# Where the weight conversions of an FNet and hard-swish kernel stand at its start: moving them behind the input's fold and beside the first steps

## The chip, the cores and the metric

One core of a Trainium2 chip. The metric is the device time of one execution in microseconds (us). Executions of one kernel here mostly agree within 0.4%; "fast" means that no execution was disturbed by a lower clock. Ratios are, throughout, the mean time of one kernel's fast runs over the mean of the kernel before's fast runs of the same rounds on the same chip, so they are not quite the ratio of the medians that stand beside them. Times within an execution ("at 100.2 us") are counted from the start of the profiled span.

## The reference

```python
X = np.fft.fft(np.fft.fft(x, axis=1), axis=2).real          # x: (8, 3008, 256) float32
h = X.reshape(24064, 256) @ w_in                            # w_in: (256, 2048) float64
g = h * np.clip(h + 3.0, 0.0, 6.0) / 6.0
out = g @ w_out                                             # w_out: (2048, 256) float64
```

The weights arrive as float64. The kernel reads them as pairs of 32-bit words and makes float32 of them itself.

## The kernel before

The batch is worked in four pairs of sequences. For the first pair this happens in order: the **fold** (eight chunks; GpSimd adds each row to its mirror row, VectorE completes the sums, TensorE applies the first transform, ScalarE copies it to `z`, which goes to DRAM); the load of `g` from there and the **second transform**; then the **steps**, each made of a first product with `w_in`, the activation on VectorE and ScalarE, a combination on GpSimd and a second product with seven matrices `G` made of `w_out`. There are eight steps to a chunk of columns and 384 in all.

The weights come in sixteen pieces, converted two at a time. Eight **conversion pairs** are numbered 0 to 7 in order of use. Pairs 0, 1, 3 and 4 belong to `w_in` and end in a product on TensorE; pairs 2, 5, 6 and 7 belong to `w_out` and end in four operations of GpSimd that fill `G`. One conversion pair goes through every engine:

```python
def narrow_a(j):
    ...
    ts(ex[:], hi, 20, 0x7FF, op0=AL.logical_shift_right, op1=AL.bitwise_and)          # VectorE
    nc.scalar.activation(exf, ex[:], AF.Relu, bias=bias[:, 0:1], scale=1.0)           # ScalarE, three times
    nc.scalar.activation(exf, exf, AF.Relu, bias=bias[:, 1:2], scale=-1.0)
    nc.scalar.activation(ex[:], exf, AF.Identity, bias=bias[:, 2:3], scale=-2.0 ** 23)
    ts(top[:], hi, 0xFFFFF, 0x100000, op0=AL.bitwise_and, op1=AL.bitwise_or)          # VectorE again
    ...
def narrow_b(j):
    st, hi, ex, frac = raw.pop(j)
    nc.vector.scalar_tensor_tensor(ex[:], hi, -2 ** 31, ex[:], op0=AL.bitwise_and, op1=AL.bitwise_or)
    o = st[:].bitcast(F32)[:, 0:WB]
    eng = nc.vector if j < 6 else nc.gpsimd
    eng.tensor_tensor(o, frac, ex[:].bitcast(F32), op=AL.mult)
    w[PIECES[j]] = o
def mix_w_out(j):                                   # a pair of w_out
    ...
    tt(g[3], b11, b12, op=AL.subtract)              # GpSimd, four times
    tt(g[5], b22, g[3], op=AL.add)
    ...
    nc.scalar.mul(g[5], g[5], -1.0)
def fold_w_in(n):                                   # a pair of w_in
    ...
    for blk in range(2):
        ps = bank([P, WB], "wps")
        for i in range(2):
            nc.tensor.matmul(ps[:], C[:, i, blk * P:(blk + 1) * P], ws[i], start=(i == 0), stop=(i == 1))
        nc.scalar.copy(W1[:, blk, cs], ps[:])
    ...                                             # and WN, from sixteen narrow matmuls
```

The main order of the start, before (cut):

```python
narrow_pair(0); use_pair(0)
for c in range(NXC):                                # the fold
    fold(first, c, 0, nc.gpsimd)
    fold(first, c, 1, nc.vector)
    if c + 3 < NXC:
        load_x(first, c + 3)                        # a direct load, then a gather of mirror rows, both on GpSimd
    if c in (2, 5):
        narrow_pair((c + 1) // 3)                   # pairs 1 and 2
    for i in range(XC // 2):
        stage1(first, c, i)
    ...                                             # loads of later pieces and of T
    if c in (2, 5):
        use_pair((c + 1) // 3)
load_g(first, 0); load_g(first, 1); load_t(1)
narrow_pair(3)
...                                                 # second transform
use_pair(3)
...                                                 # pairs 4 to 7 beside steps 0, 1, 3, 5
```

So the seven pairs after pair 0 stand in three places: **two in the fold, one in the gap** between the last `z` and the first step, **four beside the steps**. I write this as 2/1/4.

## Time and profile before

| kernel before | |
|---|---|
| time, median of 3 (range) | 2081.8 us (2078.97 to 2082.96) |
| profiled span, mean clock | 2078.6 us, 0.975 |
| fold of chunk 0 / 3 / 6 / 7 starts on GpSimd | 18.3 / 39.8 / 70.8 / 73.1 us |
| last `z` issued | 85.0 us |
| first VectorE operation of the first step ("first s") | 106.89 us |
| last GpSimd operation into `G` ("last G") | 179.11 us |
| first s to last G | 72.2 us |

The prediction shows the lines that carry this. A line of a timeline reads: start, length, engine, line of the kernel, operation, output<-input, shape, how many were merged, and in brackets the idle time of the engine before it and what ended that. Two more views matter later. The first is VectorE's timeline at the end of one chunk's fold, in the kernel before:

```profile
49.18 0.68 DVE L158 TENSOR_TENSOR y<-xt 94x508 f32<-94x508 f32 x1
49.78 2.27 DVE L159 TENSOR_TENSOR y<-xt 94x8 f32<-94x8 f32 x1
51.98 1.57 DVE L157 TENSOR_TENSOR y<-xt 94x508 f32<-94x508 f32 x1
```

An operation on 8 elements a partition took 2.27 us. The median of its eight executions on VectorE is 0.165 us. The second is the table of busy time by stretch, whose columns are stretch, length, then busy us (and instructions) of TensorE, its weight loads, VectorE, ScalarE, GpSimd, then the granted clock, the DMA share and GB/s:

```profile
100.00:130.00 30.00, 18.37 (x71) 10.65 (x70) 12.16 (x22) 10.13 (x17) 10.03 (x10) 0.82 0.22 64
130.00:165.00 35.00, 25.35 (x102) 21.19 (x101) 25.50 (x47) 17.02 (x29) 20.80 (x23) 0.86 0.25 73
```

While pairs 4 to 7 stand beside the steps, no engine is full and the clock is below 1.

A matmul is called **cold** here and in the prediction where the trace has it at about twice the time that it takes at full clock. The first half of the product at 119.88 us, after a wait of 8.62 us, took 3.97 us at a clock of 0.50; the second half, after a wait of 0.68 us, took 1.98 us at 1.00. **Full clock** is a granted clock of 1.00, as from 208 to 260 us: there four matmuls of 128x256 took 1.03 us, and two of 94x512 were 0.86 us ahead of the next operation, 0.43 each.

### The profile page before, as it was taken

The numbers are of one execution on the slowest core, as the hardware profiler recorded it, in microseconds if no ns is written. First come the engines' busy times: TensorE is split into PE (matmuls) and PEld (weight loads), VectorE is DVE, ScalarE is ACT, GpSimd is POOL, SyncE is SP. The second block draws the span as 40 slices with busy tenths as digits, with TensorE's granted clock in tenths as the row PEclk, the third lists the DMA queues.
The fourth block names the chain that finished last, engine by engine and source line by source line (L and its number), as shares of the span: only waits on it lengthen the run. The fifth ranks groups of instructions, "written<-read, shape, count | busy, mean of one in ns | idle before, by whom it ended". The sixth has DMA issues, their size and how long they took to land.

```text
span 2078.6 us, 28133 instructions
## 1 busy us (share of the span) xinstructions
PE 1974.6 (95%) x9136; PEld 1692.0 (81%) x9136; DVE 1456.9 (70%) x2714; ACT 706.1 (34%) x1205; POOL 1496.1 (72%) x1662
## 2 busy tenths in 40 slices
PE   4468999999999999999999999999999999999997
PEld 1246888888888888888888888888888888888886
DVE  5366676776777677677677677677777777777775
ACT  2344333333333333333333333333333323333332
POOL 6248777877667887788667778778766766766765
PEclk7688999999999999999999999999999999999999
DMA  6420211221110122212111112211110011011000
GB/s 188 142 86 15 57 49 34 50 47 33 29 31 23 44 51 51 51 33 54 29 21 34 43 34 48 51 43 47 31 36 11 17 23 21 18 24 21 16 16 18
DMA packets 158161, 86.81 MB, mean 42 GB/s; under 512 B 132512, under 2 KB 145056, under 8 KB 158016
## 3 DMA queue, kind: packets, MB, share of 16 engines
q1 hardware_dynamic: 129856, 60.28, 12.7%
q0 software_dynamic: 28160, 24.73, 4.5%
q8 instruction: 74, 1.21, 0.3%
q14 instruction: 71, 0.58, 0.1%
HBM read 47.65 MB, written 37.22 MB: 41 GB/s over the span
## 4 chain that ended last, share of the span: by engine, by line
PE 91%; DVE 4%; DMA 2%; ACT 1%; issue 1%; POOL 1%; SPq 0%; DVEq 0%; POOLq 0%; ACTq 0%
PE acc L320 53%; PE v L266 16%; PE u L266 15%; PE ps L193 2%; PE ps L221 2%; PE wps L446 1%; PE ps L237 1%; DVE a L298 1%; DMA st<-in_moe_w_in_dram 1%; ACT t L295 1%; DVE u L279 0%; DVE ex L406 0%; DVE s L271 0%; PE wns L451 0%; DMA g<-zd 0%
## 5 line engine op out<-in xcount | busy, mean ns | idle before, releaser
L310 POOL TENSOR_TENSOR c<-a 128x512 f32<-128x512 f32 (+1 forms) x384 | 479.2, 1248 | 406.7 <-DVE a L298 258.7
L320 PE MATMUL acc<-c,G 128*128 128x256 f32 (+1 forms) x3072 | 714.1, 375 | 0.0
L320 PEld LDWEIGHTS acc<-c,G 128*128 128x128 f32 x3072 | 579.3, 191 | 73.8 <-POOL c L310 0.2
L295 ACT ACTIVATE t<-u,half 128x512 f32<-128x512 f32 (+2 forms) x416 | 272.3, 655 | 1074.8 <-DVE u L279 1063.2
L271 DVE SCALAR_TENSOR_TENSOR s<-qn,WN,u 128x256 f32<-128x256 f32 x768 | 334.4, 477 | 392.2 <-PE u L266 391.9
L320 PE MATMUL acc<-a,G 128*128 128x256 f32 (+1 forms) x2304 | 553.6, 377 | 0.0
L320 PEld LDWEIGHTS acc<-a,G 128*128 128x128 f32 x2304 | 436.8, 191 | 57.3
L266 PE MATMUL v<-q,W 128*128 128x256 f32 x1536 | 398.8, 382 | 17.9 <-DVE a L298 17.9
L266 PE MATMUL u<-q,W 128*128 128x256 f32 x1536 | 394.5, 379 | 0.0
L266 PEld LDWEIGHTS v<-q,W 128*128 128x128 f32 x1536 | 291.3, 191 | 64.3 <-issue 21.9
L266 PEld LDWEIGHTS u<-q,W 128*128 128x128 f32 x1536 | 287.4, 190 | 65.3 <-issue 20.9
L298 DVE SCALAR_TENSOR_TENSOR a<-t,u 128x512 f32<-128x512 f32 (+2 forms) x416 | 265.9, 646 | 105.3 <-ACT t L295 101.0
L310 POOL TENSOR_TENSOR c<-a,c 128x256 f32<-128x256 f32 (+1 forms) x384 | 275.0, 716 | 30.1
L310 POOL TENSOR_TENSOR c<-c,a 128x256 f32<-128x256 f32 (+1 forms) x384 | 275.0, 716 | 30.1
L279 DVE TENSOR_TENSOR u<-s,v 128x512 f32<-128x512 f32 (+1 forms) x384 | 263.0, 685 | 42.6 <-PE v L266 2.5
L295 ACT ACTIVATE t<-v,half 128x512 f32<-128x512 f32 (+1 forms) x384 | 257.0, 669 | 5.3 <-DVE v L285 4.4
L285 DVE TENSOR_TENSOR v<-v,s 128x512 f32<-128x512 f32 (+1 forms) x384 | 257.7, 671 | 1.1
L298 DVE SCALAR_TENSOR_TENSOR a<-t,v 128x512 f32<-128x512 f32 (+1 forms) x416 | 255.1, 619 | 0.1
L310 POOL TENSOR_TENSOR r<-w,e 128x256 f32<-128x256 f32 (+1 forms) x96 | 92.3, 982 | 3.8
L193 PE MATMUL ps<-y,F 94*96 94x512 f32 x120 | 67.0, 656 | 26.2 <-DVE y L159 20.1
L326 ACT ACTIVATE e<-acc 128x512 f32<-128x512 f32 (+1 forms) x192 | 87.0, 543 | 2.9 <-PE acc L320 2.8
L346 DVE STREAM_TRANSPOSE o<-r 128x256 f32<-128x256 f32 (+1 forms) x192 | 72.4, 415 | 6.5 <-POOL r L310 6.4
(70 smaller groups left out, 826.7 us busy)
## 6 DMA issues: line engine op xcount, KB each, us to landing
out_dram<-o SPq DMA_DIRECT2D x736, 32.0 KB, 1.6
zd<-z SPq DMA_DIRECT2D x32, 384.0 KB, 3.0
g<-zd SPq DMA_DIRECT2D x48, 256.0 KB, 4.2
xt<-in_x_dram POOLq DMA_DIRECT2D x28, 376.0 KB, 3.9
st<-in_moe_w_in_dram SPq DMA_DIRECT2D x8, 512.0 KB, 4.4
st<-in_moe_w_out_dram SPq DMA_DIRECT2D x8, 512.0 KB, 5.7
T<-in_c_stage_dram SPq DMA_DIRECT2D x12, 128.0 KB, 7.2
xt<-in_x_dram POOLq DMA_DIRECT2D x4, 282.0 KB, 3.4
```

The source lines that it names most:

```text
L193: nc.tensor.matmul(ps[0:PZ], F[0:PR, 0:PZ], y[:, 2 * i:2 * i + 2, :], start=True, stop=True)
L221: nc.tensor.matmul(ps[:, blk, 2 * u:2 * u + 2], g[:, kk, blk * P:(blk + 1) * P], T[:, :, gr, blk, kk], start=True, stop=True)
L266: nc.tensor.matmul(ps[:, i], W1[:, blk, f * P:(f + 1) * P], q[:, blk, of:of + KC], start=True, stop=True)
L271: nc.vector.scalar_tensor_tensor(s[:, i].rearrange("p k n -> p (k n)"), qn[:, of * N2:(of + KC) * N2], WN[:, f:f + 1], u[:, i].rearrange(" ...
L279: nc.vector.tensor_tensor(u[:, :, 0:ns], s[:, :, 0:ns], v[:, :, 0:ns], op=AL.add)
L285: nc.vector.tensor_tensor(v[:, :, 0:nm], v[:, :, 0:nm], s[:, :, 0:nm], op=AL.subtract)
L295: nc.scalar.activation(t, h, AF.Relu, bias=half[:], scale=scale)
L298: nc.vector.scalar_tensor_tensor(dst, t, 1.0, h, op0=AL.min, op1=AL.mult)
L310: nc.gpsimd.tensor_tensor(out, in0, in1, op=AL.add)
L320: nc.tensor.matmul(ch.acc[i // 2][:, i % 2, 0:ch.n], G[:, i, fc, :], mv, start=(fc == 0 and i % 2 == 0), stop=(fc == NF - 1), skip_group_c ...
L326: nc.scalar.mul(ch.e[:, k:i + 1, 0:ch.n], ch.acc[i // 2][:, 0:i + 1 - k, 0:ch.n], 1.0 / WS)
L346: nc.vector.transpose(o[:, 0:n // DH, h], ch.r[:, m, h, 0:n].rearrange("p (j i) -> p j i", i=DH))
```

## The change

The intent: let the fold run at the speed of its loads alone. No conversion stands in it any more, only three of the weight pieces after the first pair are loaded beside it, and the direct load of `x` leaves GpSimd for SyncE, in 96 rows instead of 94. Pairs 1 and 2 move into the gap, and pair 3 moves past the first step, behind each step's own work: 0/2/5. The multiplications of pieces 2 to 5 go from VectorE to GpSimd. A changed sign of the sixth product saves ScalarE's multiplication by -1.

```diff
-PROD = ("P1", "P2", "-P4", "P5", "P7", "P6", "P3")
+PROD = ("P1", "P2", "-P4", "P5", "P7", "-P6", "P3")
@@ load_forward, the direct half of load_x
+        nr, eng = (PR + 2, nc.sync) if pr.p == 0 else (PR, nc.gpsimd)
+        rows = x_pn[pr.p * PR:pr.p * PR + nr]
@@ finish
-        add(wn[:, 0], e[:, 0], e[:, 5])
+        nc.gpsimd.tensor_tensor(wn[:, 0], e[:, 0], e[:, 5], op=AL.subtract)
@@ narrow_b
-        eng = nc.vector if j < 6 else nc.gpsimd
+        eng = nc.vector if j < 2 else nc.gpsimd
@@ mix_w_out
-        nc.scalar.mul(g[5], g[5], -1.0)
@@ the start
     for c in range(NXC):
         fold(first, c, 0, nc.gpsimd)
+        if c + 3 < NXC:
+            load_partners(first, c + 3)
         fold(first, c, 1, nc.vector)
-        if c + 3 < NXC:
-            load_x(first, c + 3)
-        if c in (2, 5):
-            narrow_pair((c + 1) // 3)
         for i in range(XC // 2):
             stage1(first, c, i)
-        for j in {0: (2, 3), 2: (4,), 3: (5,), 5: (6,), 6: (7,), 7: (8, 9)}.get(c, ()):
-            load_w(j)
+        if c + 3 < NXC:
+            load_forward(first, c + 3)
         if c == 4:
             load_t(0)
-        if c in (2, 5):
-            use_pair((c + 1) // 3)
+            load_w(2)
+        if c == 5:
+            load_w(3)
+            load_w(4)
+    narrow_pair(1)
+    use_pair(1)
     ... load_w(5), load_w(6); load_g(first, 0), load_g(first, 1), load_t(1) ...
-    narrow_pair(3)
+    narrow_pair(2)
+    use_pair(2)
     ... second transform ...
-    use_pair(3)
@@ beside the steps
-            for i, t in enumerate((0, 1, 3, 5)):
-                ... load_w, load_t, narrow_pair(4 + i), use_pair(4 + i) ahead of step t's work
+            for i, t in enumerate((0, 1, 1, 3, 4)):
+                after.setdefault(t, []).extend([(narrow_pair, (3 + i,)), (use_pair, (3 + i,))])
+                ... load_w; all of it behind step t's work
```

More of the change, by code (lines that the diff above doesn't have):

```diff
@@ L116, in __init__ @@
             self.p = p
-            self.x, self.y, self.z = {}, {}, {}
+            self.x, self.xr, self.y, self.z = {}, {}, {}, {}
             self.zd = None
@@ L125, in x_tile, with load_forward, load_partners @@
             pool, tag = ((apool, "a"), (cpool, "c"), (spool, "t"))[(i >= 8) + (i >= 11)]
-        return pool.tile([PR, XC, D], F32, tag=tag, name="xt")
+        return pool.tile([PR + 2, XC, D], F32, tag=tag, name="xt")
     def load_x(pr, c):
-        xt, xr = x_tile(pr, 2 * c), x_tile(pr, 2 * c + 1)
-        rows = x_pn[pr.p * PR:(pr.p + 1) * PR]
+        load_forward(pr, c)
+        load_partners(pr, c)
+    def load_forward(pr, c):
+        xt = x_tile(pr, 2 * c)
+        nr, eng = (PR + 2, nc.sync) if pr.p == 0 else (PR, nc.gpsimd)
+        rows = x_pn[pr.p * PR:pr.p * PR + nr]
         n = XC if c < NXC - 1 else XC - 1
-        nc.gpsimd.dma_start(out=xt[:, 0:n, :], in_=rows[:, c * XC + 1:c * XC + 1 + n, :])
+        eng.dma_start(out=xt[0:nr, 0:n, :], in_=rows[:, c * XC + 1:c * XC + 1 + n, :])
         if n < XC:
-            nc.gpsimd.dma_start(out=xt[:, n:XC, :], in_=rows[:, 0:1, :])
+            eng.dma_start(out=xt[0:nr, n:XC, :], in_=rows[:, 0:1, :])
+        pr.x[c] = xt
+    def load_partners(pr, c):
+        xr = x_tile(pr, 2 * c + 1)
+        pr.xr[c] = xr
         i = pr.p * NXC + c
         nc.gpsimd.indirect_dma_start(
-            out=xr[:].rearrange("p n d -> p (n d)"), out_offset=None, in_=x_r,
+            out=xr[0:PR].rearrange("p n d -> p (n d)"), out_offset=None, in_=x_r,
             in_offset=bass.IndirectOffsetOnAxis(ap=IX[:, i:i + 1], axis=0),
         )
-        pr.x[c] = xt, xr
     def fold(pr, c, part, eng):
-        xt, xr = pr.x[c]
+        xt, xr = pr.x[c][0:PR], pr.xr[c][0:PR]
         n = XC if c < NXC - 1 else XC - 1
@@ L165, in fold @@
             eng.tensor_copy(y[:, n, 0:P + 1:P], xt[:, n, 0:P + 1:P])
-        del pr.x[c]
+        del pr.x[c], pr.xr[c]
     starting = [True]
@@ L476 @@
         fold(first, c, 0, nc.gpsimd)
+        if c + 3 < NXC:
+            load_partners(first, c + 3)
         fold(first, c, 1, nc.vector)
-        if c + 3 < NXC:
-            load_x(first, c + 3)
-        if c in (2, 5):
-            narrow_pair((c + 1) // 3)
         for i in range(XC // 2):
             stage1(first, c, i)
-        for j in {0: (2, 3), 2: (4,), 3: (5,), 5: (6,), 6: (7,), 7: (8, 9)}.get(c, ()):
-            load_w(j)
+        if c + 3 < NXC:
+            load_forward(first, c + 3)
         if c == 4:
             load_t(0)
-        if c in (2, 5):
-            use_pair((c + 1) // 3)
+            load_w(2)
[4 more added lines that the diff above has]
+    use_pair(1)
+    for j in (5, 6):
+        load_w(j)
     load_g(first, 0)
@@ L492 @@
     load_t(1)
-    narrow_pair(3)
+    narrow_pair(2)
+    use_pair(2)
+    for j in (7, 8):
+        load_w(j)
     for i in range(2):
@@ L503 @@
     NST = 2 * NF
+    after = {}
     def beside(p):
@@ L512, in beside @@
         if p == 0:
-            for i, t in enumerate((0, 1, 3, 5)):
-                for j in (10, 11, 12, 13, 14, 15)[2 * i:2 * i + 2]:
-                    put(t, load_w, j)
-                if i + 2 < NG:
-                    put(t, load_t, i + 2)
-                put(t, narrow_pair, 4 + i)
-                put(t, use_pair, 4 + i)
+            for i, t in enumerate((0, 1, 1, 3, 4)):
+                after.setdefault(t, []).extend([(narrow_pair, (3 + i,)), (use_pair, (3 + i,))])
+                for j in range(9 + 2 * i, min(11 + 2 * i, 16)):
+                    after[t].append((load_w, (j,)))
+            for gr in range(2, NG):
+                after.setdefault(gr - 1, []).append((load_t, (gr,)))
             put(NF - 1, close_w)
@@ L573 @@
         mlp2(*chunk(s))
+        for f, a in after.get(s, ()):
+            f(*a)
         if fc == NF - 1:
```

## The prediction

> **What bounds the kernel now.** I read first the busy slices of the page (the span in 40 slices of 52 us; PE is TensorE, POOL is GpSimd, PEclk the clock granted to TensorE).
>
> ```profile
> PE   4468999999999999999999999999999999999997
> POOL 6248777877667887788667778778766766766765
> PEclk7688999999999999999999999999999999999999
> ```
>
> From the fifth slice to the last TensorE is full at full clock. The change touches nothing there, so it can only gain or lose in the first four slices. Next, the table of busy time by stretch: in 0 to 208 us TensorE is busy 124.6 us (21.7 + 25.0 + 34.5 + 43.4) at clocks of 0.74, 0.63, 0.84 and 0.87. In full-clock work there is less: by 187 us four folds of w_in (8 x 0.43 + 1.7 = 5.1 us each), 32 matmuls of the first transform (0.43 each, 13.8), the second transform (3.5), nine first halves of a step (1.73) and seven second halves (3.02): 20.5 + 13.8 + 3.5 + 15.6 + 21.1 = 74.5 us. So 187 - 74.5 = 112 us is the most a perfect start could give back. A gain over 2% needs 41.6 us of it.
>
> Where it goes is in the timeline of GpSimd, line by line (start, length, instruction, idle before and its releaser; L151 is the first instruction of a chunk's fold):
>
> ```profile
> 18.27 1.26 POOL L151 TENSOR_TENSOR xt<-xt 94x508 f32<-94x508 f32 x1 [8.06 <-DMA xt<-in_x_dram,IX]
> 39.78 1.50 POOL L151 TENSOR_TENSOR xt<-xt 94x508 f32<-94x508 f32 x1 [6.43 <-DMA xt<-in_x_dram,IX]
> 66.86 1.11 POOL L433 TENSOR_TENSOR G<-st 128x256 f32<-128x256 f32 x1 [13.85 <-DVE st L409]
> 70.83 1.25 POOL L151 TENSOR_TENSOR xt<-xt 94x508 f32<-94x508 f32 x1
> ```
>
> Chunks 0 and 3 wait for the gather of their partner rows. Chunk 6 waits in GpSimd's order behind a converted weight piece, which came late. Then TensorE's timeline around the step machinery:
>
> ```profile
> 95.44 3.75 PE L221 MATMUL ps<-T,g 128*128 128x128 f32 x16 [11.36 <-DMA g<-zd]
> 105.66 1.11 PE L266 MATMUL u<-q,W 128*128 128x256 f32 x4
> 119.88 3.97 PE L446 MATMUL wps<-st,C 128*128 128x512 f32 x4 [8.62 <-POOL st L409]
> 145.47 2.05 PE L266 MATMUL v<-q,W 128*128 128x256 f32 x4 [5.88 <-DVE a L298]
> 162.87 2.05 PE L266 MATMUL v<-q,W 128*128 128x256 f32 x4 [3.77 <-DVE a L298]
> 180.32 2.05 PE L266 MATMUL v<-q,W 128*128 128x256 f32 x4 [4.88 <-DVE a L298]
> ```
>
> The first step starts at 105.7, and each of the four pairs of weight pieces converted beside steps 0 to 5 costs TensorE a hole. The last is over at 182.2; from there it never waits. The time of the kernel is therefore the moment at which this start is over.
>
> One line of ScalarE shows what the changed sign is for: it multiplies G by -1 after GpSimd's third addition, and the step's relu stands behind it.
>
> ```profile
> 143.62 0.42 ACT L437 ACTIVATE G<-G 128x256 f32<-128x256 f32 x1 [1.57 <-POOL G L435]
> 143.94 0.67 ACT L295 ACTIVATE t<-u,half 128x512 f32<-128x512 f32 x1
> ```
>
> [...] in the undisturbed stretch from 200 to 600 us the direct 94-row load lands in a median 3.9 us, the gather of as many bytes in 11.7. So 96 rows on SyncE are harmless, and the gather stays slow. [...] four matmuls took 2.05 us after a hole against 1.03 otherwise. [...] the second L406 of a pair took 1.23 us against 0.68 while GpSimd multiplied.
>
> **The change part by part.**
>
> *Fold.* Removed ahead of the folds: weight pieces 2 and 3 (1 MB at 25 us) and the conversion of two pairs. The forward load leaves GpSimd: its issue cost 0.57 + 0.3 a chunk, so the cadence falls from 5.04 to 2.25 + 0.3 + 1.9 = 4.45 us. The gathers keep their lead of three chunks. Gather 0 was landed at 18.27 with three direct loads in its own queue; now those come behind weights in the other[...]: still 18.3. Gather 3 took 18.4 us (21.4 to 39.8)[...], 11.7 undisturbed[...], issued at 20.9, it lands at 37.0 (estimate). Chunks 3, 4, 5 fold at 37.0, 41.5, 45.9; gathers 6 and 7, issued at 39.6 and 44.0, now have pieces 2 to 4 and z beside them[...] and land at about 56.5 and 62. Fold 7 ends at 64.4 (75.3 before), VectorE at 66.3, the cold first-transform matmuls and the copy of z at 71.2 (84.7 before): **13 us gained here**.
>
> *Between fold and first step.* Before, g landed 10.7 us after z; now about 82, no longer the bound. In front stand now, one behind the other: ScalarE's six conversion activations for pair 1 (behind its z copies, 4.3 us, to 75.5); VectorE and GpSimd (2.0, to 77.6); TensorE's fold of the pair with its copies (6.7, as from 48.66 to 55.33 before, to 84.3); ScalarE's next six, behind the WN copy (4.3, to 88.6); 2.6 to the last product (91.2); four GpSimd G operations (3.0); then the Nyquist product (1.05), its matmul (1.7) and copy (0.6). Step 0's first VectorE operation starts at about 97.5 against 106.9: **9.4 us remain**.
>
> *Beside the steps.* Five pairs stand there instead of four. Before, from step 0's VectorE start to the last G operation: 179.1 - 106.9 = 72.2. Now: three steps of VectorE (11.1); pair 3: 7.4 to its last product, 7.3 to the next u, 4.8 to the end of that step on VectorE (19.5); pair 4: 7.4 + 7.3; pair 5's activations stand behind pair 4's copies on ScalarE (4.4), then 2.1 to the last product and 3.0 of G; TensorE's second half of step 2, partly cold (2.4), second-transform and mlp1 (2.1), one step on VectorE (3.7): 32.6 for 4 and 5; pair 6 with one step 10.1; pair 7 10.5. Sum 83.8. So **11.6 us lost**: one more pair (about 19.5), less the -1 and the better places of 6 and 7. The last G operation comes at 97.5 + 83.8 = 181.3, 2.2 later; the second half of step 6 then has to catch up 1.8 us less of cold clock than before (it took 4.7 us instead of 3.0).
>
> *Nothing in steady state.* A subtraction for an addition in 32 outputs on GpSimd is the same instruction and size, and GpSimd is not the bound; later pairs load and fold as before; the four removed ScalarE multiplications are 1.7 us off the path in themselves.
>
> The walk so ends within a microsecond of the kernel before: 13 - 3.6 - 11.6 + 1.8. I choose 4 us better, because the walk errs to one side: [...] I took TensorE cold in every fold. **2077 us.**
>
> **The rivals.** (a) The conversions are really hidden, and all 13 us of the fold plus the removed ScalarE waits (about 6 us) reach the end: 2060 to 2065. For it: those waits (2.5 and 3.0 us of VectorE behind relu) are real. Against it: one more pair, with a TensorE fold and a single PSUM bank, stands between steps; order on ScalarE puts activations behind copies. (b) The gather is less disturbed than I think and lands in 12 us each time: folds 6 and 7 at 50 and 55, another 7 us: 2070. Against: 18.4 us measured beside weights. (c) The long chain of conversions before step 0 becomes the bound and holds g's results; the extra fold leaves TensorE cold longer: 2085 to 2092. For it: four ScalarE groups in a row. (d) Buffers: pieces 9 to 15 wait for one of five buffers. By my times each lands 5 us or more before its use, so no wait.
>
> **Range and chances.** Fold end is good to 3 us, the chain before step 0 to 4, the one beside steps to 5; together about 7, plus 2 for run to run. 2064 to 2088 holds eight in ten. Over 2% faster would need 2040, more than all parts together give; 2% slower needs 2123.
>
> **What would show it.** In the changed profile: fold 3 starts near 37, fold 7 near 62, released by the gather, with no weight operation between; z's last write near 71. If fold 7 starts before 57, (b) holds. Step 0's first VectorE operation near 97.5, the TensorE wait before it released by GpSimd's product and not by g; if near 90, the ScalarE order was misread. The last G operation near 181; if before 170, (a) holds. TensorE full from about 185, and slices five on unchanged; were they not, the whole argument fails.

## The result, and the profile after

The changed kernel took **2092.47 us** median (2092.32 to 2092.94, 4 runs) against 2082.3 us (2078.97 to 2082.96, 4 runs) of the kernel before in the same rounds: ratio 1.0052, 95% interval 1.0035 to 1.0070. That is within 2%, as I gave it most chances to be, but about 10 us slower where I had said 5 us faster, and outside my range of 2064 to 2088. The profiled span is 2090.6 us against 2078.6.

First the busy slices of the changed kernel's page, as for the kernel before:

```profile
PE   4667999999999999999999999999999999999997
POOL 5237878788677788778667788787866766766765
PEclk7678999999999999999999999999999999999999
```

From the fifth slice on TensorE is as full as before, so the loss is in the first four. Then GpSimd's timeline, the first fold instruction of chunks 0, 3 and 7:

```profile
20.22 1.26 POOL L161 TENSOR_TENSOR xt<-xt 94x508 f32<-94x508 f32 x1 [11.11 <-DMA xt<-in_x_dram,IX]
41.07 1.25 POOL L161 TENSOR_TENSOR xt<-xt 94x508 f32<-94x508 f32 x1 [7.67 <-DMA xt<-in_x_dram]
64.99 0.99 POOL L161 TENSOR_TENSOR xt<-xt 94x381 f32<-94x381 f32 x1 [4.48 <-DMA xt<-in_x_dram]
```

Chunk 7 does fold 8 us earlier. But chunks 3 and 7 were released by the direct load (no `IX` in the bracket), not by the gather. Next, TensorE's timeline beside the steps, first the second half of the one product of the kernel before (its first half, 3.97 us, stands in the prediction):

```profile
124.52 1.98 PE L446 MATMUL wps<-st,C 128*128 128x512 f32 x4 [0.68 <-ACT W L447]
```

and then the changed kernel:

```profile
118.16 3.78 PE L455 MATMUL wps<-st,C 128*128 128x512 f32 x4 [6.87 <-POOL st L419]
122.61 3.78 PE L455 MATMUL wps<-st,C 128*128 128x512 f32 x4 [0.68 <-ACT W L456]
127.07 1.96 PE L460 MATMUL wns<-C,st 128*128 128x1 f32 x16 [0.68 <-ACT W L456]
128.89 1.11 PE L276 MATMUL u<-q,W 128*128 128x256 f32 x4
139.34 4.08 PE L455 MATMUL wps<-st,C 128*128 128x512 f32 x4 [5.46 <-POOL st L419]
150.29 1.35 PE L276 MATMUL u<-q,W 128*128 128x256 f32 x4
159.34 1.22 PE L330 MATMUL acc<-a,G 128*128 128x256 f32 x2 [0.64 <-POOL G L445]
```

Two products of `w_in` now stand there, at 118.2 and 139.3, where the kernel before had one. Each half is four matmuls in 3.7 to 4.1 us, twice the 1.98 us of the half above, and the granted clock in the four is 0.50 to 0.53. The table by stretch agrees:

```profile
100.00:130.00 30.00, 18.40 (x64) 11.16 (x63) 15.58 (x28) 9.65 (x15) 14.10 (x14) 0.77 0.10 28
130.00:165.00 35.00, 24.64 (x72) 14.78 (x72) 18.01 (x32) 13.29 (x22) 12.87 (x13) 0.66 0.35 105
```

From 130 to 165 us TensorE did 72 matmul instructions at a clock of 0.66 where the kernel before did 102 at 0.86. ScalarE's timeline shows why pair 5 was late:

```profile
150.46 0.16 ACT L462 COPY WN<-wns 128x4 f32<-128x4 f32 x1 [2.04 <-PE wns L460]
150.52 0.72 ACT L406 ACTIVATE ex<-ex,bias 128x512 f32<-128x512 int32 x1
```

Pair 5's first activation stands in ScalarE's order behind pair 4's last copy out of PSUM and starts 0.06 us after that copy starts. The relus that close a step are no longer behind a multiplication by -1.

**Where the 13.4 us of last G come from.** Last G moved from 179.11 to 192.54. The path splits into three stretches that add up:

| stretch | before | predicted | after | predicted change | measured change |
|---|---|---|---|---|---|
| start to last `z` issued | 85.0 | 71.2 | 73.9 | -13.8 | -11.1 |
| last `z` to first s | 21.9 | 26.3 | 26.3 | +4.4 | +4.4 |
| first s to last G | 72.2 | 83.8 | 92.3 | +11.6 | +20.1 |
| sum: last G | 179.1 | 181.3 | 192.5 | +2.2 | +13.4 |

The middle stretch was predicted to the tenth, the first is off by 2.7 us, and the last, beside the steps, by 8.5 us. No VectorE operation of these conversions waits for the load of a weight piece in the changed kernel's trace, so late pieces are not the reason.

### The profile page after: what moved, and what is told of

It is laid out like the page before. It is cut to its first block, busy times and chain, and to the rows that moved or that the text cites. A ratio compares the mean times of both kernels' runs of the same rounds, so it can differ in the third digit from the quotient of the medians.

```text
span 2090.6 us, 28140 instructions
## 1 busy us (share of the span) xinstructions
PE 1988.7 (95%) x9136; PEld 1692.3 (81%) x9136; DVE 1457.6 (70%) x2710; ACT 704.3 (34%) x1201; POOL 1494.2 (71%) x1657
## 4 chain that ended last, share of the span: by engine, by line
PE 89%; DVE 3%; issue 2%; ACT 2%; POOL 2%; DMA 1%; SPq 0%; DVEq 0%; POOLq 0%; ACTq 0%
PE acc L330 52%; PE v L276 15%; PE u L276 15%; PE ps L203 2%; PE ps L231 2%; PE ps L247 1%; DMA xt<-in_x_dram 1%; PE wps L455 1%; DVE a L308 1%; ACT t L305 0%; POOL st L419 0%; DVE u L289 0%; DVE s L281 0%; DMA st<-in_moe_w_in_dram 0%; DVE y L169 0%
## 5 line engine op out<-in xcount | busy, mean ns | idle before, releaser
L203 PE MATMUL ps<-y,F 94*96 94x512 f32 x120 | 74.1, 719 | 27.3 <-DVE y L169 21.2
```

The costliest lines, as they stand in the source:

```text
L203: nc.tensor.matmul(ps[0:PZ], F[0:PR, 0:PZ], y[:, 2 * i:2 * i + 2, :], start=True, stop=True)
```

## The experiments

All kernels gave correct results. Times are medians, with the ratio to the kernel before and its interval. The table comes first, because its columns read best together. "Places" counts pairs 1 to 7 in the fold, in the gap and beside the steps; the columns from chunk 7 to span minus last G are read from the one profiled execution of each kernel, which can lie some us off the median (that of y_first is the slowest of its six, 2101.6 us).

| run | places | chunk 7 folds | first s | first s to last G | last G | span minus last G | time, us | ratio (95%) |
|---|---|---|---|---|---|---|---|---|
| before | 2/1/4 | 73.1 | 106.9 | 72.2 | 179.1 | 1899.5 | 2082.3 | 1 |
| after | 0/2/5 | 65.0 | 100.2 | 92.3 | 192.5 | 1898.1 | 2092.5 | 1.0052 (1.0035 to 1.0070) |
| sign_only | 2/1/4 | 72.9 | 105.5 | 71.0 | 176.5 | 1898.2 | 2077.8 | 0.9991 (0.9977 to 1.0005) |
| x_only | 2/1/4 | 78.4 | 111.4 | 72.1 | 183.5 | 1899.4 | 2087.2 | 1.0035 (1.0021 to 1.0049) |
| no_x | 0/2/5 | 63.1 | 98.7 | 95.5 | 194.2 | 1898.2 | 2091.3 | 1.0050 (1.0037 to 1.0063) |
| y_first | 0/2/5 | 71.0 | 106.3 | 95.8 | 202.1 | 1897.7 | 2095.3 | 1.0069 (1.0055 to 1.0082) |
| fwd_ahead | 0/2/5 | 60.9 | 96.0 | 95.6 | 191.6 | 1897.9 | 2091.9 | 1.0051 (1.0039 to 1.0063) |
| lead6 | 0/2/5 | 59.9 | 102.1 | 92.5 | 194.6 | 1897.9 | 2092.0 | 1.0058 (1.0043 to 1.0074) |
| warm | 0/2/5 | 68.9 | 104.3 | 86.1 | 190.4 | 1898.1 | 2088.9 | 1.0040 (1.0026 to 1.0053) |
| interleave | 0/2/5 | 66.3 | 100.8 | 88.7 | 189.5 | 1898.1 | 2089.8 | 1.0050 (1.0036 to 1.0065) |
| pair3_early | 0/3/4 | 68.1 | 112.6 | 75.0 | 187.6 | 1897.9 | 2086.9 | 1.0025 (1.0012 to 1.0039) |
| repaired | 0/3/4 | 61.5 | 105.9 | 71.2 | 177.1 | 1898.2 | 2078.2 | 0.9987 (0.9973 to 1.0001) |
| repaired_cold | 0/3/4 | 61.9 | 106.3 | 71.3 | 177.6 | 1898.0 | 2077.4 | 0.9985 (0.9970 to 0.9999) |
| w_early | 2/1/4 | 63.1 | 103.2 | 70.9 | 174.1 | 1898.2 | 2072.8 | 0.9960 (0.9945 to 0.9974) |
| w_early_warm | 2/1/4 | 62.5 | 100.6 | 70.8 | 171.4 | 1898.0 | 2073.2 | 0.9972 (0.9958 to 0.9987) |
| w_late | 1/2/4 | 60.9 | 98.3 | 71.3 | 169.6 | 1898.0 | 2070.4 | 0.9957 (0.9943 to 0.9971) |
| w_late_push3 | 1/1/5 | 62.6 | 88.6 | 91.8 | 180.5 | 1898.0 | 2075.7 | 0.9980 (0.9966 to 0.9994) |

**Span minus last G** is 1897.7 to 1898.2 us in every kernel with the new sign and 1899.4 to 1899.5 in the two with the old one: the rest of the kernel does not change, and the profiled time is last G plus a constant. **First s to last G** is 71 to 75 us with four pairs beside the steps and 86 to 96 us with five, whatever was done to the loads.

### The parts of the change on their own: sign_only and x_only

sign_only is the kernel before with the sign alone:

```diff
-PROD = ("P1", "P2", "-P4", "P5", "P7", "P6", "P3")
+PROD = ("P1", "P2", "-P4", "P5", "P7", "-P6", "P3")
-        add(wn[:, 0], e[:, 0], e[:, 5])
+        nc.gpsimd.tensor_tensor(wn[:, 0], e[:, 0], e[:, 5], op=AL.subtract)
-        nc.scalar.mul(g[5], g[5], -1.0)
```

> The kernel before with one part of the change alone: the sixth product is taken with its sign turned, so ScalarE no longer multiplies G by -1 and a subtraction on GpSimd takes the place of an addition. Theory A (the ScalarE multiplication held relu, and with it VectorE, back behind GpSimd's third addition beside the three last pairs): VectorE's waits of 2.55 and 3.00 us before L298 fall under 1 us, each of the three pairs ends some 1.5 to 2 us earlier, 2076 to 2079 us against 2082. Rival: the pairs are paced by GpSimd's own row of products, G operations and combinations, and nothing moves: 2081 to 2083.

The ratio's interval reaches 1, but last G came 2.6 us earlier and another 1.3 us went after it. VectorE's three waits for the relu fell much as theory A had it, from 2.55, 3.00 and 2.51 us to:

```profile
141.41 0.69 DVE L298 SCALAR_TENSOR_TENSOR a<-t,u 128x512 f32<-128x512 f32 x1 [0.58 <-ACT t L295]
158.28 0.69 DVE L298 SCALAR_TENSOR_TENSOR a<-t,u 128x512 f32<-128x512 f32 x1 [1.01 <-ACT t L295]
174.87 0.69 DVE L298 SCALAR_TENSOR_TENSOR a<-t,u 128x512 f32<-128x512 f32 x1 [0.53 <-ACT t L295]
```

But of the three waits of TensorE that the prediction showed, only the first fell clearly: 2.56, 4.55 and 4.78 us instead of 5.88, 3.77 and 4.88.

So ScalarE's multiplication did hold the relu back, some 2 us each time, and yet the stretch beside the steps fell by 1.2 us only. VectorE now comes to the next pair earlier, while GpSimd still works on the step's combinations, and there its operations take longer: the first four of pair 6 took 3.96 us instead of 2.36, those of pair 7 3.84 instead of 2.87. In the times the sign is worth 0 to 4 us: the last G says 2.6, the ratio 0.09% with an interval that reaches 1.

x_only is the kernel before with its direct loads of `x` on SyncE, in 96 rows, behind each chunk's `z`:

```diff
+        nr, eng = (PR + 2, nc.sync) if pr.p == 0 else (PR, nc.gpsimd)
@@ the start
-        if c + 3 < NXC:
-            load_x(first, c + 3)
+        if c + 3 < NXC:
+            load_partners(first, c + 3)
+        fold(first, c, 1, nc.vector)
         ...
         for i in range(XC // 2):
             stage1(first, c, i)
+        if c + 3 < NXC:
+            load_forward(first, c + 3)
```

> The kernel before with the x part of the change alone: forward rows on SyncE with 96 partitions behind each chunk's z, gathers alone on GpSimd; all conversions where the kernel before has them. Theory A (fold end is set by gathers, weights and SyncE's order, and conversions inside the fold still block chunk 6): fold 7 begins at 69 to 75, no gain: 2080 to 2088, worse if forward rows wait on SyncE behind z as they do in the changed kernel (fold 3 released by them at 41). Rival (the x loads are what made the changed kernel's folds end 8 us earlier): fold 7 begins below 67 and the time is 2073 to 2077.

It loses 7 us alone, and chunk 7 folds at 78.4 us, later than either theory had it. GpSimd's timeline of this run, chunks 3 and 5:

```profile
41.94 1.25 POOL L161 TENSOR_TENSOR xt<-xt 94x508 f32<-94x508 f32 x1 [8.59 <-DMA xt<-in_x_dram]
58.67 1.25 POOL L161 TENSOR_TENSOR xt<-xt 94x508 f32<-94x508 f32 x1 [6.47 <-DMA xt<-in_x_dram]
```

Both wait for the direct load, which stands in SyncE's order behind the store of an earlier chunk's `z` and so is issued only when that `z` is ready. Chunk 5 folded at 50.7 in the kernel before.

### The fold: no_x, fwd_ahead, y_first, lead6

These four start from the changed kernel. no_x gives GpSimd its direct loads back:

```diff
-        nr, eng = (PR + 2, nc.sync) if pr.p == 0 else (PR, nc.gpsimd)
@@ the start
-        if c + 3 < NXC:
-            load_partners(first, c + 3)
         fold(first, c, 1, nc.vector)
+        if c + 3 < NXC:
+            load_x(first, c + 3)
```

> The changed kernel with its x part undone: forward rows again by GpSimd, ahead of each gather; conversions where the change has them. The x part alone added 7 us to the kernel before (2087.2 against 2080.0), its forward rows landing late behind z on SyncE. Theory A (the x part costs, and independently the moved conversions cost the rest): fold 3 begins near 37 to 39, released by the gather, fold 7 below 63, step 0's first VectorE operation 95 to 99, the last G operation 187 to 191, time 2084 to 2088, still slower than before. Rival (all of the loss is the x part): 2076 to 2081.

The time stays at 1.0050, slower than both theories had it. So the rest of the change, which is the moved conversions with their multiplications and piece loads and the sign, makes the whole loss, and the loads of `x`, which cost 7 us by themselves, add nothing to it.

fwd_ahead keeps the loads on SyncE but issues them ahead of `z`:

```diff
         if c + 3 < NXC:
             load_partners(first, c + 3)
+            load_forward(first, c + 3)
         fold(first, c, 1, nc.vector)
         for i in range(XC // 2):
             stage1(first, c, i)
-        if c + 3 < NXC:
-            load_forward(first, c + 3)
```

> The changed kernel with each forward load of x issued on SyncE ahead of the z of the same chunk instead of behind it, so that chunk 3's goes out at 5 us and the others one chunk earlier. Theory A (the forward rows on SyncE wait for z and so release folds 3, 6 and 7): these folds are then released by the gather, fold 3 at 37 to 39, fold 7 at 61 to 63, the time falls by 2 to 4, to 2088 to 2090. Rival (the gathers are no earlier, they land at the same moment): fold 3 stays at 40 to 41, no change.

It does to the fold what it should. Chunk 3 in this run's timeline of GpSimd:

```profile
35.78 1.25 POOL L161 TENSOR_TENSOR xt<-xt 94x508 f32<-94x508 f32 x1 [0.98 <-DMA xt<-in_x_dram,IX]
```

It waits for the gather again and starts at 35.8, which is even ahead of the 37.0 of my prediction. The first s came 4.2 us earlier than in the changed kernel, and the stretch beside the steps grew by 3.3. Of what was won in the fold less than 1 us reached the end. Of the 3.3, 2.4 arise up to the end of pair 3's step: there TensorE's sixteen narrow matmuls took 3.58 us in this execution and 1.96 in the changed kernel's.

y_first puts VectorE's 8-element operation at the head of its three, to keep it from meeting the gather's issue on GpSimd:

```diff
         y = ypool.tile(...)
+        tt(y[:, 0:n, 0:P + 1:P], a[:, :, 0:P + 1:P], r[:, :, 0:P + 1:P], op=AL.add)
         tt(y[:, 0:XC, 1:P], lo, hi, op=AL.add)
         tt(y[:, 0:XC, P + 1:D], lo, hi, op=AL.subtract)
-        tt(y[:, 0:n, 0:P + 1:P], a[:, :, 0:P + 1:P], r[:, :, 0:P + 1:P], op=AL.add)
```

> The changed kernel with VectorE's three operations of a chunk in another order: the one of 8 elements first instead of last. In the changed kernel it took 3.21 us for chunks 0, 1 and 4, from 1.05 us into GpSimd's gather issue to the end of GpSimd's next fold; alone it takes 0.17. Theory A (it was shut out by GpSimd's fold[...]): placed ahead of the gather's issue it takes 0.17 us, the last of the three now starts 0.75 us in and escapes too, z of chunk 0 is written near 28.5 in place of 31.4, fold 3 begins near 38.5, the time falls 2 to 3. Rival (whichever operation comes last is shut out): the 128-column operation takes 3.7 us, the time is unchanged.

A miss: neither the theory nor the rival held. VectorE's and GpSimd's timelines of this run show that the operation met the gather's issue all the same:

```profile
26.92 1.88 POOL L150 DMA_INDIRECT xt<-in_x_dram,IX  x1 [0.19 <-issue]
28.84 1.27 POOL L161 TENSOR_TENSOR xt<-xt 94x508 f32<-94x508 f32 x1
30.05 1.09 POOL L162 TENSOR_TENSOR xt<-xt 94x508 f32<-94x508 f32 x1
...
27.97 3.21 DVE L167 TENSOR_TENSOR y<-xt 94x8 f32<-94x8 f32 x1
31.18 0.68 DVE L168 TENSOR_TENSOR y<-xt 94x508 f32<-94x508 f32 x1
```

It begins 1.05 us into the issue and ends with GpSimd's second fold instruction. As the next chunk's first operation it comes at the same moment as the last of the chunk before did. The order within VectorE was not the cure, and what the operation waits for within those 3.2 us stays open.

lead6 issues six chunks at the start instead of three:

```diff
-    for c in range(3):
+    for c in range(6):
         load_x(first, c)
@@ the fold
-        if c + 3 < NXC:
-            load_partners(first, c + 3)
+        if c in (1, 2):
+            load_partners(first, c + 5)
+            load_forward(first, c + 5)
```

> The changed kernel with x really ahead: forward rows and gathers of chunks 0 to 5 are all issued at the start, those of 6 and 7 behind folds 1 and 2; piece 2 after chunk 2 and pieces 3 and 4 after chunk 3. Theory A (each gather takes 12 to 16 us wherever it stands[...], and three in flight set the pace of the folds; six in flight run beside each other): fold 0 at 21 to 24, folds 1 to 5 each 2.4 us later, fold 7 at 44 to 50 instead of 65, the first VectorE operation of step 0 some 15 us earlier, time 2074 to 2080. Rival (the DMA engines together are the limit, more gathers in flight only slow each other): fold 0 at 28 or later, fold 7 not before 58, time 2086 to 2092.

The times of the rival in my expectation held. The six gathers issued at the start took a median 28.3 us to land (chunk 0's was issued at 3.7 us and released its fold at 33.4), against 14.6 for the changed kernel's first four, and the DMA share of the first 20 us is 0.98 instead of 0.69; the direct loads, doubled as well, have a part in this that the run doesn't separate. Chunk 0 folds at 33.4 us instead of 20.2; chunk 7 gains 5 us and the first s loses 2.

### Beside the steps: pair3_early, warm, interleave

These also start from the changed kernel. pair3_early takes pair 3 back ahead of the first step (the loads of the pieces are cut from the diff):

```diff
+    stage2n_mul(first, 0)
+    narrow_pair(3)
     for i in range(2):
         stage2(first, 0, i)
-    stage2n_mul(first, 0)
     stage2n_sum(first, 0)
+    use_pair(3)
@@ beside the steps
-            for i, t in enumerate((0, 1, 1, 3, 4)):
-                ... pairs 3 + i
+            for i, t in enumerate((1, 1, 3, 4)):
+                ... pairs 4 + i
```

> The changed kernel with pair 3 of the weights converted and folded ahead of the first step, as the kernel before has it (behind the Nyquist product on GpSimd), so four pairs instead of five stand beside steps. Theory A (a pair with a TensorE fold between steps costs 22 us of the start there and only some 5 ahead of step 0, because nothing else overlaps it): the first VectorE operation of step 0 moves from 100.2 to 104 to 107, the last G operation from 192.5 to 174 to 178, and the time is 2074 to 2079, below the kernel before. Rival (the place of the pair does not matter, its chain is the same length anywhere): step 0 starts 15 to 20 us later and the time stays at 2089 to 2094.

The stretch beside the steps fell by 17.3 us, to 75.0, and the first s came 12.4 us later; some 3 us of that 12.4 were there from the fold of chunk 0 on, at 23.4 us in this execution. Half of the loss is back, and I had expected all of it.

warm runs six dummy matmuls ahead of each of the two products beside the steps, so that TensorE does not come to them out of a long wait:

```diff
             ps = bank([P, WB], "wps")
+            if blk == 0 and not starting[0]:
+                for _ in range(6):
+                    nc.tensor.matmul(ps[:], C[:, 0, 0:P], W1[:, 0, 0:WB], start=True, stop=True)
```

> The changed kernel with six extra matmuls into the same bank ahead of each of the two folds of w_in that stand beside steps; their results are overwritten. They fill the time in which TensorE waits for the conversion, so that its clock is not down when the fold comes. Theory A (the cold clock stretched these folds): from the last product of the pair to the next u 6.5 to 7.3 us in place of 9.6 and 9.0, wps of one half 1.7 in place of 3.8 us; the time falls by 4 to 6, to 2086 to 2088. Rival (the folds are paced by the single bank and ScalarE's copies, clock or not): under 1 us each, 2090 to 2092.

TensorE's timeline of this run, pair 3's product:

```profile
122.19 2.35 PE L458 MATMUL wps<-st,C 128*128 128x512 f32 x4 [1.73 <-POOL st L419]
125.21 1.98 PE L458 MATMUL wps<-st,C 128*128 128x512 f32 x4 [0.68 <-ACT W L459]
```

The halves took 2.35 and 1.98 us instead of 3.78 each, and from the pair's last multiplication to the next `u` it was 6.3 and 6.5 us (pairs 3 and 4) instead of 9.6 and 9.0, as theory A had it. The twelve matmul instructions of the six dummies took 5.31 us, 0.44 each, so they were not cold. The stretch fell by 6.2 us, but the first s of this execution came 4.0 us later (chunk 0 folded at 24.3 us), so last G moved by 2.2. The median fell by 3.5, and the ratio from 1.0052 to 1.0040.

interleave converts pairs 4 and 5 before either is used, so that pair 5's activations stand ahead of pair 4's copies on ScalarE (the loads are cut again):

```diff
-            for i, t in enumerate((0, 1, 1, 3, 4)):
-                after.setdefault(t, []).extend([(narrow_pair, (3 + i,)), (use_pair, (3 + i,))])
+            for t, ps in ((0, (3,)), (1, (4, 5)), (3, (6,)), (4, (7,))):
+                do = after.setdefault(t, [])
+                do.extend([(narrow_pair, (i,)) for i in ps] + [(use_pair, (i,)) for i in ps])
```

> The changed kernel with pairs 4 and 5 narrowed one after the other before either is put to use, so that the three activations of pair 5's exponents stand ahead of pair 4's two copies into W1 and its copy into WN on ScalarE. Theory ([...]pair 5's activations behind those copies cost 8.4 us of VectorE's wait and put the G of pair 5 late): the G end of pair 5 falls from 159.96 to 152-155 us, the last operation into G from 192.5 to 184-187, and the time to 2083-2087 us. Rival (pair 5 is bound by GpSimd's own multiplications and combinations, or the matmul engine): the last operation into G stays within 2 us of 192.5 and the time at 2090-2093 us.

The first half of the expectation held: pair 5's `G` was complete at 152.1 us instead of 160.0. But last G moved by 3.1 us only and the time hardly. TensorE's timeline of this run shows the wait that took the place of the other:

```profile
146.60 3.78 PE L455 MATMUL wps<-st,C 128*128 128x512 f32 x4 [2.35 <-ACT W L456]
151.06 3.58 PE L460 MATMUL wns<-C,st 128*128 128x1 f32 x16 [0.68 <-ACT W L456]
154.49 2.05 PE L276 MATMUL u<-q,W 128*128 128x256 f32 x4
```

Pair 4's copy now stands behind pair 5's activations, its product ends 4.2 us later, and the next step's `u` with it (154.5 against 150.3).

### All together, and without the dummies: repaired and repaired_cold

repaired is the changed kernel with fwd_ahead, pair3_early, interleave and the dummy matmuls; repaired_cold leaves the dummies out. The main lines of the diff:

```diff
+            load_forward(first, c + 3)              # ahead of z, as in fwd_ahead
+    narrow_pair(3)                                  # ahead of the first step, as in pair3_early
+    use_pair(3)
-            for i, t in enumerate((0, 1, 1, 3, 4)):
+            for t, ps in ((1, (4, 5)), (3, (6,)), (4, (7,))):
```

> The changed kernel with all four repairs: forward loads ahead of each z, pair 3 converted before the steps, pairs 4 and 5 narrowed before either is used, six dummy matmuls ahead of the first half of pair 4's product. If the parts of the loss that I named are the whole of it and add up: first s at 106-109 us, the last operation into G at 173-178, the time 2072-2078 us, thus 0-10 us below the kernel before. Rival (conversion work beside the steps costs more than before the steps for a reason not yet named, so that each repair shifts it only): the last operation into G at 182-188 us, 2083-2088 us.

> The run repaired without the six dummy matmuls. Theory of the cold clock: the first half of pair 4's product is 3.6-4.1 us instead of 2.2, but its second half was cold in repaired too (3.78, after a wait for ScalarE), so it is 1-3 us longer than repaired: 2079-2081 us. Rival (the dummies only take time): the same or shorter than repaired, 2075-2078 us.

repaired came to 2078.2 us and last G to 177.1, at the upper edge of what the first theory had: the parts that I had named make up the whole loss against the kernel before. By ratio pair3_early, fwd_ahead, interleave and warm alone give 0.27%, 0.01%, 0.02% and 0.12%, and the four together 0.65%. That they help each other is likely, since what fwd_ahead wins in the fold is lost beside the steps as long as five pairs stand there; but the ratios, each good to about 0.15%, do not show it. repaired_cold is no slower (2077.4). So here the dummies bring nothing. The first half of pair 4's product was not cold in repaired (two times 1.12 us, for two matmuls each) and cold in repaired_cold (4.08 us), but the second half has to wait for ScalarE in both, starts 27.8 us after the first s in both, and is cold in both (3.78 us).

### A version that beats both kernels: w_early, w_early_warm, w_late, w_late_push3

w_early starts from sign_only and moves only the use of pair 2 behind chunk 7's fold, with its second piece loaded one chunk earlier:

```diff
-        for j in {0: (2, 3), 2: (4,), 3: (5,), 5: (6,), 6: (7,), 7: (8, 9)}.get(c, ()):
+        for j in {0: (2, 3), 2: (4, 5), 5: (6,), 6: (7,), 7: (8, 9)}.get(c, ()):
-        if c in (2, 5):
-            use_pair((c + 1) // 3)
+        if c in (2, 7):
+            use_pair(1 if c == 2 else 2)
```

> The kernel before with the new sign and without the -1 multiply; in addition its loads of weight pieces 4 and 5 both come at chunk 2 and pair 2's combinations of w_out (four GpSimd operations) stand behind chunk 7's fold, so that chunk 6's fold no longer waits for them. My theory (one span of conversion work, wherever it stands, costs the same; only idle time of GpSimd and the fold chain can be saved): fold 6 moves from 70.6 us to 57-62 us, the last z load from 84.8 to 73-76, the first s from 105.5 to 96-101, the last operation into G from 176.5 to 168-173, the stretch between stays at 71-73 us, and the time falls to 2068-2074 us. Rival: the work before the steps (pairs 2 and 3) is itself the limit and the first s stays at 104-106: then 2076-2079 us, no gain over the sign change alone.

The time came as expected, 2072.8 us, but the last `z` moved only to 81.7 and the first s to 103.2, so the number was met with part of the path missed: pair 2's VectorE work still stood ahead of chunk 6's (60.4 to 70.2 us). w_early_warm adds the dummies to it:

> As the run with pair 2's combinations behind chunk 7, and six dummy matmuls ahead of the first half of a w_in product beside the steps (pair 4 alone here). Theory of the cold clock: the product's first half falls from 3.8-4.0 us to about 2.0-2.4 and the rest of this pair ends 1-2 us earlier; the time falls by 0-2 us against the run without. Rival: the dummies themselves ([...]about 6 x 1 us, while GpSimd is still multiplying) take the matmul engine from the step's own products and it is 1-3 us longer.

They did nothing that the times show (2073.2 us), and the theory's step did not happen either: the product's first half took 3.83 us instead of 3.96. The dummies were not cold here either (5.31 us, not the 6 that the rival feared) and were over at 110.2 us, and TensorE then stood idle for 3.43 us before the product; in warm it was 1.73 and 0.31 us.

w_late, again with the new sign, moves all of pair 2 behind chunk 7's fold, and nothing past the first step (cut: piece 5 is loaded one chunk earlier, piece 8 one chunk earlier and piece 9 behind `load_g`):

```diff
-        if c in (2, 5):
-            narrow_pair((c + 1) // 3)
+        if c == 2:
+            narrow_pair(1)
         for i in range(XC // 2):
             stage1(first, c, i)
+        if c == 2:
+            use_pair(1)
+        if c == 7:
+            narrow_pair(2)
+            use_pair(2)
```

> The kernel before with the new sign, with pair 2 converted and used behind chunk 7's fold (in the run w_early only its use was moved, and its VectorE work still stood ahead of chunk 6's: 60.4 to 70.2 us, so z came at 81.7). Theory (only conversion work pushed past the first step costs; up to the load of g it is free): fold 7 at 60-64 us, the last z at 71-75 (81.7 in w_early), the first s at 97-102 (103.2), the last operation into G at 168-173 (174.1), the time 2066-2071 us. Rival (moving conversions out of the fold costs as such, because pairs 2 and 3 then stand one behind the other ahead of the first step): the first s at 103-106 us and the time 2073-2078 us, no better than w_early.

Every number of the theory held. This kernel has the lowest median, 2070.4 us (2069.36 to 2074.22, 5 runs), ratio 0.9957, though w_early's interval (0.9945 to 0.9974) does not part it from that one. GpSimd's and VectorE's timelines of this run:

```profile
58.54 1.26 POOL L151 TENSOR_TENSOR xt<-xt 94x508 f32<-94x508 f32 x1 [5.90 <-DMA xt<-in_x_dram,IX]
...
98.30 0.87 DVE L271 SCALAR_TENSOR_TENSOR s<-qn,WN,u 128x256 f32<-128x256 f32 x2 [12.68 <-PE u L266]
```

Chunk 6 waits for its gather alone and folds 12.3 us earlier than in the kernel before, and the first step starts 8.6 us earlier (7.2 earlier than in sign_only). The fold's gain is real as long as it is not paid for behind the first step.

w_late_push3 adds that one thing, pair 3 past the first step (the loads of pieces, which follow it, are cut):

```diff
-    narrow_pair(3)
     ... second transform ...
-    use_pair(3)
@@ beside the steps
-            for i, t in enumerate((0, 1, 3, 5)):
-                ... narrow_pair(4 + i), use_pair(4 + i)
+            for j, t in ((3, 0), (4, 1), (5, 1), (6, 3), (7, 5)):
+                put(t, narrow_pair, j)
+                put(t, use_pair, j)
```

> The run w_late with pair 3 pushed past the first step: pairs 3 to 7 at steps 0, 1, 1, 3 and 5. Theory (a pair ahead of the first step lies beside the load of g and the second transform, a pair beside the steps stands as a hole of its own): the first s comes 5-9 us earlier than in w_late (90-93 us against 98.3), but from there to the last operation into G it takes 12-22 us more (83-93 us against 71.3), the last operation into G at 176-184 us, the time 2077-2085 us. Rival (the place of a pair does not matter, only the number of conversions still to do): the last operation into G within 3 us of 169.6 and the time 2068-2073 us.

The first s came 9.7 us earlier, at 88.6 (a little earlier than expected), and the stretch behind it took 20.6 us more: last G at 180.5 as expected. The two products in TensorE's timeline of this run look like those of the changed kernel:

```profile
101.61 4.02 PE L445 MATMUL wps<-st,C 128*128 128x512 f32 x4 [8.57 <-POOL st L409]
126.26 4.08 PE L445 MATMUL wps<-st,C 128*128 128x512 f32 x4 [5.34 <-POOL st L409]
```

The median is 5.3 us above w_late's, which is less than the theory's 7 to 15. The profiled execution was the slowest of its five (2080.3), that of w_late the fastest of its five, so the trace's 10.9 us of last G overstate what the medians show. The direction is settled, since all five executions are slower than all five of w_late; the size is about 5 us by the medians and the ratios.

## Why the prediction was wrong

Point by point, in its own order:

- **What bounds the kernel** held. Slices five on are unchanged, and span minus last G is constant to half a microsecond in all kernels with the new sign.
- **The fold** was mis-sized by 2.7 us: -11.1 instead of -13.8. The step that failed is "96 rows on SyncE are harmless". On SyncE the load stood behind `z`, was issued only when that `z` was ready (chunk 3's at 31.8 us), and so released chunks 3, 6 and 7. It did not land more slowly: from 20 to 60 us a median 8.6 us, against 9.0 in the kernel before (the 3.9 that I used is of an undisturbed stretch). My landing times of the gathers (37.0, 56.5 and 62) were estimates, 16 to 18 us from the issue, between the 11.7 us of an undisturbed gather and the 18.4 us of gather 3. My chunk 0 "still 18.3" came at 20.2. That holds for all runs: chunk 0 folds at 20.2 to 24.4 us in the nine kernels that issue three direct loads on SyncE at the start, and at 18.1 to 19.9 in the seven that issue them on GpSimd. The run fwd_ahead shows that with the load ahead of `z` chunk 3 folds at 35.8, chunk 7 at 60.9 and the last `z` goes out at 69.8, all ahead of the 37, 62 and 71.2 that I wrote. What 96 rows do against 94 no run shows.
- **Between fold and first step** held: 26.3 us predicted and measured, and the chain is the one that I named (TensorE's wait before the first step, 8.70 us, was released by GpSimd's product and not by `g`). That it fits to the tenth is luck: TensorE's part for pair 1 took 6.1 us instead of 6.7 and pair 2's last multiplication came 0.5 us sooner, while the end behind the last G operation took 4.8 instead of 3.35.
- **Beside the steps** is the step that failed, by 8.5 us. I wrote that one more pair costs about 19.5, "less the -1 and the better places of 6 and 7", and so 11.6. One more pair does cost that: +20.1 here and +20.6 in w_late_push3. The deduction of 8 us was not there: sign_only shortens the stretch by 1.2 us only, since the waits for the relu do go but come back as slower VectorE operations (3.96 and 3.84 us instead of 2.36 and 2.87), and of the better places nothing is seen (the 20.1 contain them and the new sign's 1.2, and the 20.6 are for a pair alone). In the terms of my walk it was pair 3 at 22.5 us instead of 19.5, pairs 4 and 5 at 36.1 instead of 32.6, and the end of pair 7 at 12.7 instead of 10.5. In the first two most of the difference is cold matmuls: I had 7.3 us from the last piece's multiplication to the next u, with one cold half, and measured 9.6 and 9.0 with both halves at 3.7 to 4.1 us. The run warm brought these two down to 6.3 and 6.5. In pair 7 it is VectorE again: its first four operations took 4.1 us instead of the 1.8 of pair 6, at the time of GpSimd's combinations (180.2 to 183.4 us). (The terms for pairs 4 and 5 add up to 32.4, not 32.6; that changes nothing.)
- **"I choose 4 us better, because the walk errs to one side"** failed in sign. The gathers were a little quicker than I had written (in fwd_ahead chunks 3 and 7 waited for theirs and folded at 35.8 and 60.9 us, not 37 and 62), but the walk erred more to the other side. My walk without it ended at 2081; with the 2.7 and 8.5 us it ends at 2092. The two do not count alike: fwd_ahead took the 2.7 back and the time stayed.
- **The rivals.** (a) fell. (c) came within 0.5 us of the time with its 2085 to 2092, and had half of the reason: the chain before step 0 is the bound, but no longer than I had counted; the extra product is cold, but behind the first step (granted clock 0.66 from 130 to 165 us instead of 0.86). (b) fell: the gathers took a median 15.2 us. (d) did not come into play, as no conversion beside the steps waits for its piece.

What the runs put in its place: a pair of conversions has a price by its place. In the fold, pair 2 cost 12 us of the last `z` (85.0 to 72.8 in w_late, where three pieces' loads move with it). Pair 1 cost hardly anything there: in no_x, which takes it out as well and leaves the loads of `x` as they were, the last `z` goes out at 72.0. No run moves pair 1 alone. In the gap a further pair costs 4 to 11 us, as it lies partly beside the way of `z` to DRAM and back as `g` (last `z` to first s: 14.1 us with pair 2 there in w_late_push3, 21.9 with pair 3 in the kernel before, 25.5 and 26.3 with two pairs in w_late and the changed kernel, 35.1 with three in repaired). Behind the first step it costs 20 us in the trace. The change took pair 2 out of the fold, where it was dear, and with it pair 1, where it was all but free, and paid by moving pair 3 from the gap to the dearest place.

What stays open: what exactly holds VectorE's 8-element operation for 3.2 us; why chunk 0 folds later with the direct loads on SyncE; and what the multiplications moved from VectorE to GpSimd do, which no run takes back alone (they belong to pairs 1 and 2, thus to the gap, where the prediction held).

## What to carry to other kernels

When work is moved off a start-up path, ask where it lands. Work that passes through every engine in turn was cheap here beside a round trip to DRAM (4 to 11 us a pair) and dear between short dependent steps (20 us), where in the changed kernel TensorE waited 6.87 and 5.46 us for it and then did four matmuls in 3.78 and 4.08 us at a granted clock of 0.50. Add up the stretches between a few fixed moments of the trace, before and after. If one of them is the walk's largest term and carries a deduction for "better places", measure the deduction alone before believing it: a wait that is removed can come back at the next meeting of two engines, as in sign_only, where three waits of 2.5 to 3.0 us fell to 0.5 to 1.0 and the stretch by 1.2 us only.
